# The first head's row of maxima, issued by ScalarE instead of SyncE

## The chip, the cores and the metric

One core of one Trainium2 chip runs the whole kernel. The metric is device time in microseconds (us) of one execution. Below, PE is TensorE, DVE VectorE, ACT ScalarE, POOL GpSimd and SP SyncE; "SPq" in a row is an instruction of SP's queue.

## The reference

Block-causal attention over 8 batches and 8 heads (576 positions, head size 64, blocks of 64), and then a gated product of four weight matrices:

```python
scores = scale * np.matmul(q, k.transpose(0, 1, 3, 2))        # [8, 8, 576, 576]
scores = np.where(block_i >= block_j, scores, -1000000000.0)   # blocks of 64 positions
scores = scores - np.max(scores, axis=-1, keepdims=True)
attn = np.exp(scores)
attn = attn / (np.sum(attn, axis=-1, keepdims=True) + 1e-09)
x = (attn @ v) as [4608, 512]
a = x @ w1                                                     # w1, w2: [512, 1024]
b = x @ w2
out = (a * b @ w3) @ w_out                                     # [1024, 1024], [1024, 512]
```

q, k and v are float32; the weights come as 64-bit numbers.

## The kernel before, in words

The heads are worked off in 32 pairs: four pairs for each batch, `NPAIR` = 4 and `NN` = 32. The two heads of a pair are j = 0 and 1; in tiles of 128 partitions, head j has 64 partitions of its own (`own[j]`) and uses the other 64 (`oth[j]`) for a second copy and for constants. Products are made in pieces of lower precision: each operand is split into a high and a low part.

**Scores.** For each head, the tile `qk[j]` has four slots of 576 columns. On the head's own partitions they hold q high, q low, k low, k high. On the other partitions, slots 0 and 2 get a copy of q high and k high by a transfer (L284, `qk<-qk`), and slots 1 and 3 constants (`const_rows`, L555: the mask's rows and a row of ones). A score tile (`s_tile`, L310, tile `s`) is two matmuls that add up: slot 2 times slot 0, then slot 3 times slot 1. One row of slot 1, on the partition `oth[j].start`, holds minus the maximum of every position's scores; met by the row of ones in slot 3, it subtracts the maximum within the second matmul. ACT then takes the exponential from PSUM (L318 in the first four pairs, tile `pe`; L325 to L330 later), and PE multiplies by v (L350 early, L374 later, tile `x`).

**The row of maxima.** `shift_mask(n)` makes it for pair n: PE multiplies a bf16 copy of q and k (`qd`, `kb`, L221 and L223; matmuls L235 into `mx`), DVE takes maxima of the rows (L239 to L244, tile `m`), PE transposes them (L246, `mt`), ACT negates them into `ms`, a tile of 9 partitions by 128 columns (L248). `shift(n, j)` (L257, `qk<-ms`) then moves head j's 9 by 64 numbers into the row of 576 in `qk[j]`, in 9 pieces of 256 bytes. For the first pair, n = 0, both heads' rows are moved right after each other at the end of `shift_mask`; for later pairs the second head's row follows in `prep_qk`.

**Weights.** While the first four pairs (`EARLY`) run, the weights are fetched in 21 pieces of 1 MB, in the order of `W_ORDER` ("o" is w_out, "3" is w3, "s" a piece of w1 or w2), into three raw buffers in turn (`fetch`, L184: `graw` and `wraw`). `assemble` turns the 64-bit numbers into float32: one pass on ACT (L195) and three on DVE (L196 to L198). A raw buffer is fetched into again only when its conversion is done. PE multiplies w3 by w_out once into one matrix (`gen_product`, L490, tile `w`). The gated product runs in blocks of 512 positions (`gen_moe`: L514 `ab`, then L533 `o`), filled in between the attention's steps, and continues after the last pair.

**The order of the work.** Two strings for each pair (`EARLY_PLAN`, `PLAN`) say in which order the steps are written down: S a score tile, V a part of the product with v, M a step of the next pair's maxima, A and B of preparing q and k, C a weight conversion, W a step of the product of weights, N, T and Q the end of a head. All transfers are issued from SP, in one queue. From the start to `start.close()` all five engines keep the order of the code (`manual_schedule`); this is the opening of pair 0 with its maxima, `const_rows`, the first conversion and `prep_qk`. After that a planner in the compiler orders each engine's instructions by priority and by times that it reckons for them. From pair 4 on PE keeps the order of the code again.

In the opening, the transfers on SP are: q and k of pair 0, constants, v, a first 1 MB piece of w_out, head 0's copies (L284), a first piece of w3, the two rows of maxima (L257), head 1's copies, a second piece of w3. ACT's order there is: `qd` for head 1, the high parts of head 0 (L280), `const_rows(0)`, `ms`, the first pass of the conversion (L195), v of head 0 (L296), the high parts of head 1 (L280); the first exponentials follow.

Of the kernel before, what the change touches and what calls it, by code (L numbers as in the profile page):

```python
# [7 lines left out]
F32 = mybir.dt.float32  # L8
# [10 lines left out]
BLK = 64  # L19
NB = S // BLK  # L20
# [57 lines left out]
def block_causal_attention__then__gated_mlp_kernel(ctx, tc, qkv, consts, ident_in, w1, w2, w3t, wout, out_t):  # L78
    nc = tc.nc
# [136 lines left out]
    ms_of = {}  # L216

    def shift_mask(n):
# [29 lines left out]
        nc.scalar.mul(out=ms[0:NB], in_=mt[0:NB, 0:P], mul=-1.0)  # L248
        ms_of[n] = ms
        shift(n, 0)  # L250
        if n == 0:
            shift(n, 1)
        yield

    def shift(n, j):
        row = qk[j][oth[j].start : oth[j].start + 1, 1, :].rearrange("p (i r) -> p i r", r=BLK)
        nc.sync.dma_start(out=row.bitcast(F32), in_=ms_of[n][0:NB, j * BLK : (j + 1) * BLK].bitcast(F32))  # L257

    def prep_qk(n, j):
        rqk = rqk_of[n].rearrange("p (t s) -> p t s", t=2)  # L260
        o, x = own[j], oth[j]
        if j == 1 and n:
            shift(n, 1)
        high, low = qk[j][o, 0::3, :], qk[j][o, 1:3, :]
        if n > EARLY:
            if j == 0:
                hf = tl["late"].tile([P, RQK], F32R, tag="hf", name=f"hf{n}")
                hf_of[n] = hf
                nc.scalar.copy(hf, rqk_of[n])  # L269
                yield  # L270
                lo = rqk_of[n].bitcast(F32R)
                nc.gpsimd.tensor_tensor(out=lo, in0=rqk_of[n], in1=hf, op=ALU.subtract)  # L272
                yield
            hf = hf_of[n].bitcast(F32).rearrange("p (t s) -> p t s", t=2)
            nc.sync.dma_start(out=high.bitcast(F32), in_=hf[o])
            nc.sync.dma_start(out=qk[j][x, 0::2, :].bitcast(F32), in_=hf[o])
            nc.sync.dma_start(out=low.bitcast(F32), in_=rqk[o])
            yield
            return
        nc.scalar.copy(high, rqk[o])  # L280
        yield
        if j == 0 and n:
            yield
        nc.sync.dma_start(out=qk[j][x, 0::2, :].bitcast(F32), in_=high.bitcast(F32))  # L284
        if n == 0:
            yield
        nc.vector.tensor_tensor(out=low, in0=rqk[o], in1=high, op=ALU.subtract)  # L287
        yield
# [416 lines left out]
```

## Time and profile before

| | us |
|---|---|
| median of 3 runs | 959.41 |
| lowest and highest | 957.72, 959.47 |
| the profiled execution's own time | 961.2 |
| its span, from first to last instruction | 959.4 |
| PE busy | 935.8 |
| DVE busy | 609.5 |
| ACT busy | 565.5 |

The mean granted clock of PE was 0.996 of full speed. In a row of the timeline the first number is the start, the second the length, then engine, line, operation, written and read tiles, how many were merged, and in brackets the engine's idle time before it and what ended that. A row of the chain of waits has start, length, and the work or transfer; a transfer's length there runs from its issue until the waiting engine could go on.

### The profile page before, as it was taken

What the parts mean: (1) busy time and instruction counts of PE and PEld (TensorE: products, weight loads), DVE (VectorE), ACT (ScalarE), POOL (GpSimd) and SP (SyncE); (2) the same over time, 40 slices, a digit from 0 to 9 for tenths busy, and PEclk for the clock granted to TensorE, in tenths of its full rate; (3) what the DMA queues carried; (4) which work ended last, traced back from release to release, by engine and by line L of the source; (5) the groups of instructions that cost most, each with busy time, mean ns of one, the idle gap of its engine ahead of it and who ended that gap; (6) DMA issues with size and microseconds to landing.
All of it is one profiled execution on the core that took longest, in us unless ns stands there. A gap on an engine that the chain in (4) does not pass through costs nothing.

```text
span 959.4 us, 13392 instructions
## 1 busy us (share of the span) xinstructions
PE 935.8 (98%) x4608; PEld 749.1 (78%) x4608; DVE 609.5 (64%) x1289; ACT 565.5 (59%) x1275; POOL 307.6 (32%) x254
## 2 busy tenths in 40 slices
PE   5899989999999999999999999999999999999998
PEld 3455567788888888888888888888888888888886
DVE  6899969766776677766776777667676776210010
ACT  5777666666666666666666666666666665222121
POOL 0000134352334234533453334334443443223120
PEclk9999989999999999999999999999999999999999
DMA  8788434455445544455445544554455442000001
GB/s 271 249 279 250 139 79 113 102 124 140 107 110 124 146 113 113 113 146 124 114 100 143 122 108 99 137 133 112 103 129 129 107 108 60 22 1 33 12 1 44
DMA packets 48823, 111.68 MB, mean 116 GB/s; under 512 B 5866, under 2 KB 14186, under 8 KB 48756
## 3 DMA queue, kind: packets, MB, share of 16 engines
q1 hardware_dynamic: 48756, 110.84, 44.4%
q8 instruction: 36, 0.59, 0.3%
q14 instruction: 31, 0.25, 0.1%
HBM read 50.51 MB, written 9.44 MB: 62 GB/s over the span
## 4 chain that ended last, share of the span: by engine, by line
PE 92%; DVE 3%; DMA 2%; ACT 2%; issue 1%; SPq 0%; DVEq 0%; ACTq 0%
PE ab L514 39%; PE o L533 21%; PE s L310 10%; PE x L374 9%; PE w L490 5%; PE mx L235 4%; PE x L350 3%; DMA rqk<-in_qkv 1%; DMA graw<-in_w3t 1%; DMA qk<-ms 0%; PE tot L391 0%; PE mt L246 0%; DVE m L242 0%; ACT qd L223 0%; DVE qk L287 0%
## 5 line engine op out<-in xcount | busy, mean ns | idle before, releaser
L523 POOL TENSOR_TENSOR gl<-a,gh 128x512 fp32r<-128x512 f32 x72 | 94.5, 1313 | 242.2 <-ACT gh L522 242.2
L310 PE MATMUL s<-qk 128*128 128x288 f32 (+4 forms) x768 | 158.8, 312 | 7.9 <-DMA qk<-ms 3.0
L310 PEld LDWEIGHTS s<-qk 128*128 128x128 f32 (+1 forms) x768 | 124.8, 182 | 41.1 <-issue 12.2
L242 DVE TENSOR_REDUCE m<-mx 128x1 f32<-128x512 f32 (+6 forms) x256 | 125.5, 503 | 30.9 <-PE mx L235 29.7
L329 ACT ACTIVATE ph<-s 128x448 fp32r<-128x448 f32 x224 | 85.9, 384 | 68.7 <-PE s L310 60.9
L521 DVE TENSOR_TENSOR a<-ab,a 128x512 f32<-128x512 f32 x72 | 49.6, 689 | 107.0 <-PE ab L514 104.4
L533 PE MATMUL o<-gh,wh 128*128 128x512 f32 x288 | 117.3, 407 | 0.0
L331 DVE TENSOR_TENSOR pl<-s,ph 128x448 fp32r<-128x448 f32 x168 | 81.5, 485 | 54.8 <-ACT s L330 54.4
L327 DVE TENSOR_TENSOR pl<-rsum,ph 128x288 fp32r<-128x288 f32 x112 | 56.5, 527 | 89.2 <-ACT ph L326 89.0
L533 PE MATMUL o<-gl,wh 128*128 128x512 f32 x288 | 112.8, 392 | 0.0
L533 PE MATMUL o<-gh,wl 128*128 128x512 f32 x288 | 112.6, 391 | 0.0
L272 POOL TENSOR_TENSOR rqk<-rqk,hf 128x1152 fp32r<-128x1152 f32 x27 | 72.2, 2673 | 86.8 <-ACT hf L269 86.2
L332 DVE TENSOR_TENSOR rsum<-s,rsum 128x448 f32<-128x448 f32 x224 | 92.9, 415 | 1.7
L374 PE MATMUL x<-ph,vs 128*128 128x128 f32 x336 | 87.5, 313 | 0.3 <-DVE ph L331 0.3
L522 ACT CAST gh<-a 128x512 fp32r<-128x512 f32 x72 | 44.4, 616 | 70.6 <-DVE a L521 69.5
L300 POOL TENSOR_TENSOR vs<-rv,vs 128x320 fp32r<-128x320 f32 x56 | 49.1, 878 | 113.2 <-ACT vs L299 108.0
L330 ACT ACTIVATE s<-s 128x448 f32<-128x448 f32 x224 | 85.4, 381 | 0.0
L235 PE MATMUL mx<-kb,qd 128*128 128x512 bf16 (+5 forms) x320 | 69.6, 295 | 6.9 <-DVE qd L223 5.2
L518 ACT COPY a<-ab 128x512 f32<-128x512 f32 x72 | 42.2, 586 | 55.0 <-PE ab L514 39.9
L374 PE MATMUL x<-pl,vs 128*128 128x128 f32 x280 | 71.3, 320 | 0.0
L374 PEld LDWEIGHTS x<-ph,vs 128*128 128x128 f32 x336 | 61.7, 190 | 12.2 <-DVE ph L331 3.2
L533 PEld LDWEIGHTS o<-gl,wh 128*128 128x128 f32 x288 | 54.0, 188 | 12.1
(128 smaller groups left out, 2094.3 us busy)
## 6 DMA issues: line engine op xcount, KB each, us to landing
qk<-hf SPq DMA_DIRECT2D x108, 288.0 KB
rqk<-in_qkv SPq DMA_DIRECT2D x31, 576.0 KB
qk<-rqk SPq DMA_DIRECT2D x54, 288.0 KB
rv<-in_qkv SPq DMA_DIRECT2D x31, 320.0 KB
out_t<-o SPq DMA_DIRECT2D x36, 256.0 KB
graw<-in_w3t SPq DMA_DIRECT2D x6, 1024.0 KB
graw<-in_w SPq DMA_DIRECT2D x5, 1024.0 KB
graw<-in_wout SPq DMA_DIRECT2D x3, 1024.0 KB
```

What stands on the lines that cost most here:

```text
L235: nc.tensor.matmul(sc, qd[:, i, :], kb[:, a:b], start=True, stop=True)
L242: nc.vector.reduce_max(m[:, col : col + 1], sc, axis=AX.X)
L272: nc.gpsimd.tensor_tensor(out=lo, in0=rqk_of[n], in1=hf, op=ALU.subtract)
L310: nc.tensor.matmul(t[ks, at : at + q1 - q0], qk[j][:, 2 + s, kr], qk[j][:, s, q0:q1], start=(s == 0), stop=(s == 1))
L329: nc.scalar.activation(h, sc, AF.Exp, scale=SCALE)
L330: nc.scalar.activation(sc, sc, AF.Exp, scale=SCALE)
L331: nc.vector.tensor_tensor(out=low, in0=sc, in1=h, op=ALU.subtract)
L332: nc.vector.tensor_tensor(out=r, in0=sc, in1=r, op=ALU.add)
L374: nc.tensor.matmul(xps[:, to : to + w], v[:, c, :], parts[s][:, a : a + w], start=(u < 2 and s == 0), stop=((u, s) in ((0, 1), (len(PV) - ...
L514: nc.tensor.matmul(acc[i], l[:, c, fs], r[c], start=(c == 0 and s == 0), stop=(c == NC - 1 and s == 2))
L523: nc.gpsimd.tensor_tensor(out=gl[f // 4][:, f % 4], in0=a32, in1=gh[f // 4][:, f % 4], op=ALU.subtract)
L533: nc.tensor.matmul(t, l[:, f, es], r[f // 4][:, f % 4], start=(f == 0 and s == 0), stop=(f == NF - 1 and s == 2))
```

## The change

`shift` picks the queue: for pair 0 and head 0 (`n + j == 0`) ACT issues the transfer, in all other cases SP as before. What is moved, from where and to where, is the same. In ACT's code the issue stands right after the instruction that makes `ms`.

```diff
     def shift(n, j):
         row = qk[j][oth[j].start : oth[j].start + 1, 1, :].rearrange("p (i r) -> p i r", r=BLK)
-        nc.sync.dma_start(out=row.bitcast(F32), in_=ms_of[n][0:NB, j * BLK : (j + 1) * BLK].bitcast(F32))
+        queue = nc.scalar if n + j == 0 else nc.sync
+        queue.dma_start(out=row.bitcast(F32), in_=ms_of[n][0:NB, j * BLK : (j + 1) * BLK].bitcast(F32))
```

## The prediction

> **What bounds the kernel now.** I read the page first, then PE's busy time in stretches, then the chain of waits through the opening, then the queues of SP, PE, ACT and DVE around 10 us, and last what the DMA engines moved there.
>
> ```profile
> span 959.4 us, 13392 instructions
> PE 935.8 (98%) x4608; PEld 749.1 (78%) x4608; DVE 609.5 (64%) x1289; ACT 565.5 (59%) x1275; POOL 307.6 (32%) x254
> ```
>
> PE is busy 98% of the span; a change that adds no matmul can win only PE's idle time, 959.4 - 935.8 = 23.6 us. The stretches say where it is idle (start:end, length, then busy us of PE, PEld, DVE, ACT, POOL, the granted clock, DMA share, GB/s):
>
> ```profile
> 48.00:60.00 12.00, 12.00 (x49) 7.05 (x49) 12.00 (x16) 8.48 (x15) 0.00 (x0) 1.00 0.99 294
> 60.00:80.00 20.00, 20.00 (x68) 10.50 (x66) 18.69 (x29) 14.02 (x23) 0.00 (x0) 1.00 0.68 221
> ...
> 100.00:120.00 20.00, 19.97 (x71) 10.96 (x69) 19.94 (x22) 13.48 (x24) 4.47 (x3) 1.00 0.34 118
> 200.00:500.00 300.00, 300.00 (x1590) 252.21 (x1589) 208.71 (x488) 195.37 (x472) 121.09 (x100) 1.00 0.50 121
> ```
>
> From 48 us on PE has hardly a gap. So whatever the change wins counts only if PE's matmul at about 48 us starts earlier; from there a shift is carried to the end. The chain of waits in that opening (start, length, what):
>
> ```profile
> 10.30 0.28 ACT ms L248
> 10.60 4.75 DMA qk<-ms
> ...
> 15.49 0.59 PE s L310
> 16.11 0.42 ACT pe_first L318
> ...
> 33.30 8.04 DMA graw<-in_w3t
> ...
> 47.78 1.13 PE w L490 x2
> ```
>
> The row of maxima is 4.75 us under way, and the chain runs through it. Farther on it leaves attention and runs through a fetch of w3 (33.30) and the conversion of those weights to PE's product with them at 47.78.
>
> **Why the row is late.** SP's queue, PE, and what the DMA engines moved from 12 to 16 us, in 40 slices of 0.1 us:
>
> ```profile
> 6.89 0.59 SPq L184 DMA_DIRECT2D graw<-in_w3t  x1
> 10.60 1.61 SPq L257 DMA_DIRECT2D qk<-ms  x2
> 13.96 0.68 SPq L284 DMA_DIRECT2D qk<-qk  x1
> 14.68 0.59 SPq L184 DMA_DIRECT2D wraw_first<-in_w3t  x1
> ```
>
> ```profile
> 12.80 0.82 PE L310 MATMUL s<-qk 128*128 128x288 f32 x2 [2.54 <-DMA qk<-qk]
> 15.49 0.82 PE L310 MATMUL s<-qk 128*128 128x288 f32 x2 [1.87 <-DMA qk<-ms]
> ```
>
> ```profile
> GB/s 358 348 358 389 317 328 241 197 220 192 133 108 102 46 20 31 20 20 31 20 31 20 20 31 20 20 15 0 0 0 0 0 92 161 346 138 253 138 253 184
> ```
>
> Ahead of the row on SP's queue stands a 1 MB fetch of w3, issued at 6.89. The rate falls from 350 GB/s to 46 at 13.4, as DMA engine after DMA engine finishes; then about 20 GB/s go on until 14.65, which I take for a single late engine, and 0.7 us after that stops the row is there (15.35). I read it so: the row's share on the late engine stands in that queue behind the fetch, and every share of the row must land. PE has done its first products of both score tiles by 12.80 + 0.82 = 13.62 and then waits 1.87 us for the row.
>
> **The change part by part.** Removed from SP: one issue, the first of two (1.61 us together, 0.8 each). The second head's row then issues at 10.60 rather than 11.4; still behind the fetch, it lands near 15.35, and nobody needs it before the second head's scores, which follow the whole of the first head. Nothing else on SP moves by this: its next DMA (13.96) waits for ACT's cast L280. Worth zero, covered by that wait.
>
> Added on ACT: that issue, behind `ms`, which ends at 10.58. No new instruction waits for it except the scores that waited already. ACT's queue, with what stands behind it:
>
> ```profile
> 11.29 1.12 ACT L195 ACTIVATE wbits_first<-graw 128x1024 f32<-128x1024 f32 x1 [0.72 <-DMA graw<-in_wout]
> ...
> 12.78 1.15 ACT L280 CAST qk<-rqk 64x1152 fp32r<-64x1152 f32 x1
> ...
> 21.01 1.16 ACT L195 ACTIVATE wbits<-wraw_first 128x1024 f32<-128x1024 f32 x1
> 22.74 0.64 ACT L399 COPY sm<-x 64x576 f32<-64x576 f32 x1 [0.57 <-PE x L350]
> ```
>
> ACT issues no DMA in this trace, so its price is bounded: not below 0.35 (the shortest issue of SP below), at most twice the 0.85 of SP's longest for this form, 1.70.
>
> ```profile
> L116 SPq DMA_DIRECT2D rqk<-in_qkv x4: 350/403/459, 0.7 to 26.2; - x4
> L257 SPq DMA_DIRECT2D qk<-ms x4: 709/772/850, 10.6 to 44.4; - x4
> ```
>
> I take 0.85, the same form: 10.60 + 0.85 = 11.45, so L195 starts 0.16 later (ends of the range: 0 and 10.60 + 1.70 - 11.29 = 1.01). The 0.72 us in which ACT waited for its weights covers the rest. The 0.16 passes to L280 (ends 14.09) and to SP's issue at 13.96; ACT is free before the first exponential, which comes at 13.62 + (16.11 - 15.49) = 14.24.
>
> Gained: on another queue the row doesn't stand behind the fetch. How early it lands is unknown: at the earliest like SP's idle queue at 13.96, whose bytes begin to flow at 15.2, 1.3 us later, with 0.7 to land: 10.60 + 1.3 + 0.7 = 12.6; at the latest as now, 15.35. Any time up to 13.62 does the same. I take that, as the late engine has only to put one 256-byte share between the fetch's: PE's second products start at 13.62, 1.87 us earlier. If the row is as late as now, the gain here is 0.
>
> The Trainium skill, DMA: Bandwidth & Descriptors, under Queues, rings and completion order, says that each DMA engine takes turns between the queue rows that have work, a packet (some 9 to 17 descriptors) at a time. By that the row would land near the early end, and the first rival below would have next to no chance; I leave it 15%, as no run here yet shows two queues at once.
>
> **What is late next.** From 16.11 to 20.7 nothing on ACT or PE waits for a transfer, so 1.87 is carried to about 19. Then ACT reaches L195 on `wraw_first` (21.01, would be 19.14), a weight fetch that SP issued at 14.68. When did it land?
>
> ```profile
> 15.00:16.00 1.00, 0.51 (x2) 0.50 (x2) 0.97 (x2) 0.00 (x0) 0.00 (x0) 1.00 0.70 157
> 16.00:17.00 1.00, 0.74 (x3) 0.42 (x2) 1.00 (x1) 0.87 (x3) 0.00 (x0) 1.00 1.04 204
> 17.00:18.00 1.00, 1.00 (x4) 0.96 (x4) 0.05 (x1) 1.00 (x2) 0.00 (x0) 1.00 0.90 261
> 18.00:20.00 2.00, 2.00 (x6) 1.03 (x6) 0.59 (x1) 2.00 (x4) 0.00 (x0) 1.00 1.13 390
> ...
> 15.28:32.40 17.12, 15.62 (x55) 9.63 (x55) 13.61 (x16) 13.62 (x23) 0.00 (x0) 1.00 0.98 342
> 32.40:35.20 2.80, 2.38 (x10) 1.23 (x9) 2.80 (x6) 2.25 (x4) 0.00 (x0) 1.00 0.33 94
> ```
>
> ```profile
> wraw_first<-in_w3t SPq DMA_DIRECT2D x1, 1024.0 KB
> qk<-qk SPq DMA_DIRECT2D x1, 288.0 KB
> qk<-ms SPq DMA_DIRECT2D x1, 2.2 KB
> ```
>
> The queue holds qk and w3, 1312 KB or 1.34 MB, from 15.2 (the row itself has 2.2 KB). By 18 us 157 + 204 + 261 = 622 KB have moved; the remaining 0.72 MB take 1.85 us at 390 GB/s: 19.85, and 0.7 to land, 20.5. A late engine adds to that, and it was there by 21.01. I take the middle, 20.75, plus 0.16 from ACT's issue: 20.9. L195 then ends at 20.9 + 1.16 = 22.07, and `sm` starts there rather than at 22.74: of 1.87 us some 0.67 are left. The DMA engines are full from 15.28 to 32.40 (0.98), so earlier issues bring nothing earlier there.
>
> ```profile
> 27.88 1.17 ACT L195 ACTIVATE wbits<-graw 128x1024 f32<-128x1024 f32 x1
> ...
> 32.03 1.21 DVE L198 SCALAR_TENSOR_TENSOR wo<-graw,wbits 128x1024 int32<-128x1024 int32 x1
> ```
>
> ACT then works without a gap up to L195 at 27.88 (its rows show no idle time from 22.74), and DVE converts those weights until 33.24, which frees the buffer for the fetch at 33.30. At this fetch the DMA engines had run empty (0.33 from 32.40), so it starts and lands 0.67 earlier, and so does PE at 47.78.
>
> **Sum.** +0 (SP) - 1.87 (PE's wait) + 1.20 (the wait for `wraw_first` that takes its place, ACT's 0.16 in it) = -0.67 us. The profiled execution took 961.2 us, with a span of 959.4; the median of the runs shown is 959.41. Against its own time 960.5, against the median 958.7. About 0.2%, 1.9 us, is what a measurement of this kernel can tell from no change, so the likeliest outcome is no measurable change.
>
> **The rivals.** *The row is as late as before* (15%). For it: the same 16 DMA engines move it, and the late one has to do the fetch anyhow. Against: nothing but its place in the queue explains 4.75 us for so few bytes. Then -0 + 0.16: 959.6. The Trainium skill, same page, under Issuing engines are not separate DMA queues, says that queues share the engines and a second issuer saves issue time alone; by that this row, already the first of SP's two, would win nothing. The trace here neither shows nor excludes it.
>
> *The whole 1.87 us arrives, and a little more* (17%, faster). PE waits between 15.5 and 48 us:
>
> ```profile
> PE w L490 <- DVE w L198: 2.0, 1, 2.0
> PE s L310 <- DMA qk<-ms: 1.9, 1, 1.9
> ...
> PE w L490 <- DVE wo L198: 0.4, 1, 0.4
> ```
>
> If `wraw_first` lands by about 19.3, or the planner puts `sm` ahead of it, 1.87 reaches 33.30, and the 0.4 at wo can go too: 959.4 - 2.3 = 957.1. Against: the byte count above. The most it could be is the waits shown, 4.3 us: 955.1.
>
> *The planner takes another order* (17%, slower). Only the opening up to `start.close()` is fixed on all engines by the code; behind it the planner orders instructions by times that it reckons itself, and a transfer moved from SP to ACT changes those. The place is ACT between 22.74 and 27.88, which has no gap: one L195 (1.16 us) taken ahead of the attention work, and its conversion on DVE (0.69 for L196 and twice the 1.21 of L198, at which I take L197 too, 3.1 us) ahead of the masks' maxima, delay PE by up to 3.1: 959.4 - 0.67 + 3.1 = 961.8. It decides from 2.6 us on. For it: DVE and ACT are the full engines there; against: PE holds other work to fill in.
>
> ```profile
> 19.41 0.69 DVE L196 TENSOR_SCALAR wbits<-wbits 128x1024 int32<-128x1024 int32 x1 [2.36 <-ACT wbits L195]
> ```
>
> **How the numbers follow.** Forecast 51% (958.7), row as late 15% (959.6), both without measurable change; faster 17%, slower 17%. So faster 0.17, same 0.66, slower 0.17. The range reaches from the faster rival to near the slower, 957.0 to 961.4. The forecast alone has 957.8 to 959.7: with `wraw_first` at 20.5 and no cost on ACT 0.9 + 0.16 gained and half a microsecond of spread, with 1.01 on ACT 0.2 lost.
>
> **What would show it.** Right: a DMA issue on ACT near 10.6; PE's second products at 13.6, no wait for qk<-ms there; ACT L195 on `wraw_first` still near 20.9 and now waiting for its DMA; the fetch of 33.30 at 32.6; PE w L490 at 47.1. Wrong: PE still waits for qk<-ms until 15.4; `sm` at 20.9; or a changed order of instructions after 18 us, with more idle time of PE between 22 and 131 us.

## The result, and the profile after

The changed kernel is slower: 966.60 us (median of 4 runs, 964.70 to 967.81) against 959.44 us (957.72 to 961.45) for the kernel before on the same chip, a ratio of 1.0072 [1.0052, 1.0091], 7.2 us. The prediction said 958.7 us, with a range up to 961.4, and gave "slower" 17%.

The profiled execution of the changed kernel took 964.7 us, 1.9 us less than its median, and that of before 1.8 us more than its own. So the two traces differ by only 3.5 us: they show where the time goes, the runs how much it is. (The granted clock was 0.998 in this execution and 0.996 in the other three runs; by an estimate, 0.002 of 965 us, the clock can make up to 1.9 us of the difference.) The first lines of the page after (29 matmul records are missing from this trace):

```profile
span 962.9 us, 13365 instructions
PE 935.2 (97%) x4579; PEld 747.2 (78%) x4608; DVE 610.2 (63%) x1289; ACT 566.2 (59%) x1275; POOL 308.4 (32%) x254
```

PE's idle time is 962.9 - 935.2 = 27.7 us, before it was 23.6. By stretches (columns as in the prediction), first before, then after:

```profile
16.00:48.00 32.00, 28.32 (x94) 15.37 (x93) 27.01 (x36) 23.70 (x38) 0.00 (x0) 1.00 0.83 276
48.00:100.00 52.00, 52.00 (x186) 28.30 (x186) 49.89 (x72) 38.52 (x65) 0.00 (x0) 1.00 0.85 263
100.00:200.00 100.00, 95.10 (x445) 70.65 (x444) 82.34 (x155) 67.09 (x148) 35.16 (x26) 0.97 0.41 104
```

```profile
16.00:48.00 32.00, 28.06 (x88) 15.52 (x89) 25.59 (x33) 22.06 (x36) 0.00 (x0) 0.95 0.83 274
48.00:100.00 52.00, 49.92 (x178) 26.71 (x178) 47.51 (x65) 37.46 (x63) 0.00 (x0) 1.00 0.78 246
100.00:200.00 100.00, 92.87 (x427) 66.70 (x429) 85.06 (x157) 67.90 (x146) 35.38 (x25) 1.00 0.42 110
200.00:500.00 300.00, 300.00 (x1584) 252.34 (x1596) 207.43 (x488) 195.25 (x474) 118.11 (x97) 1.00 0.50 120
```

From 48 to 100 us PE had no gap and now has 2.1 us of them; from 100 to 200 its idle time grows from 4.9 to 7.1; from 200 to 500 PE has no gap in either. From 16 to 100 us DVE and ACT are busy less: they get less done in the same time.

The opening, ACT's queue after (ACTq is an issue by ACT):

```profile
10.67 1.41 ACTq L258 DMA_DIRECT2D qk<-ms  x1
12.12 1.12 ACT L195 ACTIVATE wbits_first<-graw 128x1024 f32<-128x1024 f32 x1 [1.49 <-issue]
...
13.60 1.15 ACT L281 CAST qk<-rqk 64x1152 fp32r<-64x1152 f32 x1
15.65 0.89 ACT L319 ACTIVATE pe_first<-s 128x288 f32<-128x288 f32 x2 [0.89 <-PE s L311]
17.26 0.97 ACT L319 ACTIVATE pe_first<-s 128x448 f32<-128x448 f32 x2 [0.72 <-PE s L311]
18.79 0.43 ACT L319 ACTIVATE pe_first<-s 128x192 f32<-128x192 f32 x2 [0.56 <-PE s L311]
19.25 1.15 ACT L556 CAST qk<-cst 64x1152 fp32r<-64x1152 f32 x1
20.31 0.45 ACT L297 COPY ve<-rv 128x320 f32<-128x320 f32 x1
20.67 1.12 ACT L195 ACTIVATE wbits<-graw 128x1024 f32<-128x1024 f32 x1
```

PE's queue after, for the first score tiles:

```profile
11.33 0.58 PE L311 MATMUL s<-qk 128*128 128x288 f32 x1 [1.00 <-DMA qk<-qk]
15.03 2.73 PE L311 MATMUL s<-qk 128*128 128x288 f32 x7 [3.12 <-DMA qk<-ms]
```

Two things are to be seen. The row of maxima, issued by ACT at 10.67, is still late: PE waits for it until 15.03 (15.49 before). And the order has changed. PE does one first product and then wants the row, where before it did the first products of two tiles ahead of it. (The length of the wait, 3.12 us against 1.87, differs from execution to execution: here PE's first product starts at 11.33, before at 12.80. In a second trace of the changed kernel, that of `changed_again` below, it starts at 13.43, and the wait is 1.54 us.) On ACT all exponentials of the first head stand ahead of the constants for the second head (L556). Before, the constants and L195 stood between them:

```profile
16.11 0.71 ACT L318 ACTIVATE pe_first<-s 128x288 f32<-128x288 f32 x2 [2.17 <-PE s L310]
16.84 1.15 ACT L555 CAST qk<-cst 64x1152 fp32r<-64x1152 f32 x1
...
18.26 1.12 ACT L195 ACTIVATE wbits<-graw 128x1024 f32<-128x1024 f32 x1
19.28 0.84 ACT L318 ACTIVATE pe_first<-s 128x320 f32<-128x320 f32 x2
```

What that does shows on SP's queue. First before, then after:

```profile
18.02 0.35 SPq L116 DMA_DIRECT2D rqk<-in_qkv  x1
...
60.24 0.38 SPq L184 DMA_DIRECT2D wraw<-in_w  x1
...
128.43 0.44 SPq L116 DMA_DIRECT2D rqk<-in_qkv  x1
```

```profile
20.43 0.35 SPq L116 DMA_DIRECT2D rqk<-in_qkv  x1
21.35 0.38 SPq L184 DMA_DIRECT2D graw<-in_wout  x1
35.49 0.37 SPq L184 DMA_DIRECT2D graw<-in_w3t  x1
63.83 0.38 SPq L184 DMA_DIRECT2D wraw<-in_w  x1
134.98 0.45 SPq L116 DMA_DIRECT2D rqk<-in_qkv  x1
```

The fetch of pair 1's q and k (L116) goes into the buffer that holds the constants (`cst` and pair 1's `rqk` have the same tag in the same pool, so one buffer), so it can't start before ACT has read them for the last time. In both traces it starts 0.03 us after that cast ends: 16.84 + 1.15 = 17.99 and 18.02; 19.25 + 1.15 = 20.40 and 20.43. The view of SP's waits (after) puts this wait down to the copy of v that follows on ACT, which ended only at 20.31 + 0.45 = 20.76 and so can't have been it:

```profile
SPq L116 <- ACT ve L297: 4.6, 1, 4.6
```

The fetches of weights stand behind it in SP's queue: that of w3 goes from 33.30 to 35.49 (+2.2), the one at 60.24 to 63.83 (+3.6), and q and k at 128.43 to 134.98 (+6.6). SP's queue is not the only chain that is late, though. The conversion pass L195 on the first piece of w3 stands behind the same exponentials on ACT and starts at 20.67 instead of 18.26 (+2.4); its data had landed at 14.54. A raw buffer is fetched into again only after its conversion, so a late conversion delays fetches as well. PE comes to feel it where it needs converted w_out, 2.35 us where before it waited 0.42:

```profile
35.47 3.06 PE L491 MATMUL w<-wo,w_first 128*128 128x512 f32 x4 [2.35 <-DVE wo L198]
```

### The profile page after: what moved, and what is told of

Read it like the earlier page. It is cut to its first block, busy times and chain, and to the rows that moved or that the text cites. A ratio compares the mean times of both kernels' runs of the same rounds, so it can differ in the third digit from the quotient of the medians.

```text
span 962.9 us, 13365 instructions
## 1 busy us (share of the span) xinstructions
PE 935.2 (97%) x4579; PEld 747.2 (78%) x4608; DVE 610.2 (63%) x1289; ACT 566.2 (59%) x1275; POOL 308.4 (32%) x254
## 4 chain that ended last, share of the span: by engine, by line
PE 82%; DVE 2%; ACT 1%; issue 0%; DVEq 0%; ACTq 0%
PE ab L515 40%; PE o L534 21%; PE x L375 9%; PE s L311 9%; PE mx L235 3%; PE tot L392 0%; PE mt L246 0%; DVE rsum L333 0%; DVE a L522 0%; DVE pl L328 0%; DVE pl L332 0%; ACT ph L330 0%; DVE late_bits L197 0%; DVE late_bits L198 0%; DVE w2l L214 0%
## 5 line engine op out<-in xcount | busy, mean ns | idle before, releaser
L235 PE MATMUL mx<-kb,qd 128*128 128x64 bf16 (+7 forms) x291 | 58.3, 286 | 7.7 <-DVE qd L223 5.2
```

Source lines behind the costliest of these rows:

```text
L235: nc.tensor.matmul(sc, qd[:, i, :], kb[:, a:b], start=True, stop=True)
```

## The experiments

Two theories were put against each other: the time is lost by what the transfer itself does on ACT (its issue price), or by the order in which the planner now puts the instructions of the first four pairs. Comparing the two kernels' instructions engine by engine, PE's order differs in 149 places, DVE's in 56, ACT's within its first 121 instructions, SP's within its first 46; POOL's is the same, and nothing differs behind about 120 us.

To set the order by hand, the experiments chain the instructions of PE, DVE, ACT and SP by ordering edges without semaphores, from a list of instruction numbers for each engine. Line numbers in them are those of before.

**The changed kernel again**, with no edit.

```diff
 (the diff of the change, nothing else)
```

> The changed kernel itself, on the same chip as the three kernels beside it. Both theories: ratio 1.005 to 1.009 to the kernel before.

966.96 us, ratio 1.0072 [1.0052, 1.0092]. The loss repeats.

**The change with the order of before.**

```diff
-        nc.sync.dma_start(out=row.bitcast(F32), ...
+        (nc.scalar if n + j == 0 else nc.sync).dma_start(out=row.bitcast(F32), ...
...
+    for engine, numbers in ORDER.items():     # the order of the kernel before, 4 engines
+        for pair_ in zip(numbers, numbers[1:]):
...
+                tc.add_manual_dep(traced[b], traced[a].name, NOSYNC, reason="order")
```

> The changed kernel (the first head's row issued by ACT) with every engine's instructions held in the order that they have in the kernel before. If the planner's new order is what costs the time, this is within 1 us of before: ACT's issue takes 1.41 us, so its first conversion pass starts 0.8 us later, the row lands near 14.9 instead of 15.35, and the two nearly cancel (958.5 to 960.5). If ACT's issue itself costs the time, most of the 7 us stays: 963 to 967.

960.35 us, ratio 1.0004 [0.9996, 1.0013]: no loss, with the transfer on ACT.

```profile
10.64 1.31 ACTq L257 DMA_DIRECT2D qk<-ms  x1
11.99 1.12 ACT L195 ACTIVATE wbits_first<-graw 128x1024 f32<-128x1024 f32 x1 [1.38 <-issue]
```

```profile
15.14 0.82 PE L310 MATMUL s<-qk 128*128 128x288 f32 x2 [1.83 <-DMA qk<-ms]
```

The issue costs 1.31 us here and L195 starts 0.70 later than before (0.83 in the changed kernel), and PE's wait for the row is 1.83 instead of 1.87. Neither shows in the time. Nor does the chaining by edges, which this kernel has too.

**The order of the changed kernel, both rows on SP.**

```diff
+ORDER = {PE: ..., DVE: ..., ACT: ..., SP: ...}     # the order of the changed kernel; shift as before
```

> The kernel before (both rows issued by SP) with every engine's instructions held in the order that they have in the changed kernel. If the planner's order costs the time, this is as slow as the changed kernel, 964 to 968, ratio about 1.007. If ACT's issue costs it, this is within 1 us of before.

967.86 us, ratio 1.0082 [1.0068, 1.0097]. The loss comes without the change. The four cases together:

| | order of before | order of the changed kernel |
|---|---|---|
| first row on SP | 1 | 1.0082 [1.0068, 1.0097] |
| first row on ACT | 1.0004 [0.9996, 1.0013] | 1.0072 [1.0052, 1.0092] |

Its trace, whose execution took 2.0 us more than its median, has gaps in the same stretch, 3.3 us of them:

```profile
48.00:100.00 52.00, 48.72 (x168) 26.15 (x168) 45.88 (x63) 35.52 (x61) 0.00 (x0) 0.97 0.73 232
```

**The issue price alone: the second head's row, for which PE doesn't wait at that time, on ACT.**

```diff
-        nc.sync.dma_start(out=row.bitcast(F32), ...
+        (nc.scalar if n == 0 and j == 1 else nc.sync).dma_start(out=row.bitcast(F32), ...
+ORDER = ...                                        # the order of before
```

> The order of before, the first head's row issued by SP as before, and the second head's row, which nobody waits for at that time, issued by ACT instead: the price of the issue on ACT alone. ACT's L195 near 11.29 starts about 0.8 us later. If the order is the cause of the slower time: 0 to 0.8 us slower, 959.4 to 960.2. If ACT's issue is the cause: 963 to 967.

960.78 us, ratio 1.0014 [1.0002, 1.0025]. The issue takes 1.31 us again; it may cost 0.1%, about what can be told apart, and at most about a third of the loss by the upper end of the interval (0.25 of 0.72%).

**Which part of the order: pair 0 (to about 45 us) or what follows.**

```diff
+ORDER = ...     # both rows on SP; the changed kernel's order in pair 0, before's after it
```

> Both rows on SP, as before. Every engine has the changed kernel's order up to the end of the first pair (about 45 us) and the order of before from there. If the first pair's order carries the loss: the fetches of weights are 2.1 to 2.4 us late from 18 us on, as in the changed kernel's trace, and 2 to 2.5 us (ratio 1.002 to 1.003) arrive at the end. If the loss arises in later pairs' order: within 1 us of before. If all of it is in the first pair: 966 to 968.

964.35 us, ratio 1.0046 [1.0029, 1.0063]: more than the 0.2 to 0.3% expected. A part of it may be the clock. These six runs had a granted clock of 0.993 to 0.995, the 23 of before 0.996 to 0.998; by the means, 0.9945 and 0.9967, that is an estimated 2.1 us of the 4.4. Why their clock was lower was not found.

```diff
+ORDER = ...     # both rows on SP; before's order in pair 0, the changed kernel's after it
```

> Both rows on SP. Every engine has the order of before up to the end of the first pair (about 45 us) and the changed kernel's order from there: the other half of new_to_45us, which was 0.46% slower. If the two halves of the new order each carry a part of the loss and the parts add up: ratio 1.002 to 1.005, 2 to 4.5 us slower. If the later order costs only because the first pair came late: within 1 us of before.

963.64 us, ratio 1.0038 [1.0022, 1.0053]. Each half loses, and the halves add up: 0.46 + 0.38 = 0.84% against 0.82% for the whole order. PE's waits from 16 to 200 us in the second half's kernel show small ones (in all, times, longest) of which before has 0.2 us:

```profile
PE x L350 <- ACT pe L318: 1.7, 5, 0.5
PE mx L235 <- DVE m L242: 1.4, 2, 1.2
```

**Seven instructions of ACT alone.** Before's order with the constants, v's copy and L195 (176, 181, 185) moved behind the exponentials of the first head (212, 216, 243, 244), as the changed kernel has them; the three other engines as before.

```diff
-        ... 197, 204, 176, 181, 185, 216, 212, 243, 244, 220, ...
+        ... 197, 204, 212, 216, 243, 244, 176, 181, 185, 220, ...
```

> Both rows on SP and the order of before, but for seven instructions of ACT near 17 us, which have the changed kernel's order: the exponentials of the first head's last score tiles go ahead of the second head's constants, v and the second conversion pass (L555, L296, L195). If this place delays the chain of weights: the load of pair 1's q and k (18.0 us in before) issues near 20, the second conversion pass starts 2 us later, and 1.5 to 2.5 us arrive at the end. If those 2 us are made up before 48 us: within 1 us of before.

963.61 us, ratio 1.0037 [1.0024, 1.0050]: most of what pair 0's order costs (0.46%), and more than the 1.5 to 2.5 us expected. The rows of ACT, of SP, of PE's waits from 16 to 130 us, and two of the chain of waits, from an execution 2.0 us above the median:

```profile
20.00 1.15 ACT L555 CAST qk<-cst 64x1152 fp32r<-64x1152 f32 x1
21.41 1.12 ACT L195 ACTIVATE wbits<-graw 128x1024 f32<-128x1024 f32 x1
```

```profile
21.18 0.36 SPq L116 DMA_DIRECT2D rqk<-in_qkv  x1
...
36.56 0.37 SPq L184 DMA_DIRECT2D graw<-in_w3t  x1
```

```profile
PE w L490 <- DVE w_first L198: 3.8, 1, 3.8
PE w L490 <- DVE w L198: 2.4, 1, 2.4
```

```profile
24.55 1.24 DVE w_first L198
25.83 3.50 PE w L490 x4
```

The constants end at 21.15, SP's fetch of q and k starts at 21.18, and what stands behind it on SP is late: w3 by 3.3 us. So the place of one 1.15 us cast on ACT, before or behind the exponentials, sets when SP's queue goes on. PE then waits 6.2 us for converted weights, where before it waited 2.0 + 0.4; 3.8 us more, and the median is 3.1 us longer (by the ratio 3.6). But the longer of these waits, 3.8 us, is not SP's: it is for the conversion of the first piece of w3, whose pass L195 is one of the seven instructions and starts at 21.41 instead of 18.26, on data that SP had fetched well before the constants (issue at 7.03). So the loss belongs to the seven together; how it divides between the late conversion pass and the late queue was not separated.

**Is the row late because of the fetch ahead of it?** Both rows on SP, the 1 MB fetch of w3 issued behind them.

```diff
-        ... 133, 165, 166, 177, ...      # SP: fetch of w3, the two rows, the second head's copies
+        ... 165, 166, 133, 177, ...      # the order of before otherwise
```

> Both rows on SP and the order of before, but the fetch of w3 that stood ahead of them on SP's queue (6.89 us in before) now stands right behind them. If the row was late for standing behind that fetch: it lands by 13.3, and PE's second products start at about 13.5. If such a transfer takes 4.75 us by itself: still 15.3. The fetch comes 3 to 4 us later and what stands behind it some 1 to 1.5 us, so the time moves little: 958.5 to 961.

960.47 us, ratio 1.0000 [0.9987, 1.0013].

```profile
12.85 1.30 PE L310 MATMUL s<-qk 128*128 128x288 f32 x4 [2.40 <-DMA qk<-qk]
```

```profile
18.56 1.12 ACT L195 ACTIVATE wbits<-graw 128x1024 f32<-128x1024 f32 x1 [1.55 <-DMA graw<-in_w3t]
22.69 1.14 ACT L195 ACTIVATE wbits<-wraw_first 128x1024 f32<-128x1024 f32 x1 [1.60 <-DMA wraw_first<-in_w3t]
```

PE's wait for the row is gone: four products run on from 12.85. And nothing is gained, since ACT now waits 1.55 us for the fetch that was put back and 1.60 us for the next one.

**The row on ACT and the fetch behind the other row.**

```diff
+        (nc.scalar if n + j == 0 else nc.sync).dma_start(out=row.bitcast(F32), ...
-        ... 133, 165, 166, 177, ...      # SP
+        ... 166, 133, 177, ...           # 165 on ACT, the order of before otherwise
```

> The first head's row on ACT, the order of before, and the fetch of w3 behind the second head's row on SP. If a row on ACT's queue waits for transfers that SP issued before it, its late landing (about 14.9 in the changed kernel) goes with the fetch: 10.6 + 1.35 for ACT's issue + 1.3 + 0.7 = 14.0 or earlier. If it is ACT's own queue that is slow: still 14.9. Time 959 to 962.

959.88 us, ratio 0.9994 [0.9982, 1.0005].

```profile
12.86 0.82 PE L310 MATMUL s<-qk 128*128 128x288 f32 x2 [0.81 <-DMA qk<-ms]
```

```profile
21.66 1.13 ACT L195 ACTIVATE wbits<-wraw_first 128x1024 f32<-128x1024 f32 x1 [1.31 <-DMA wraw_first<-in_w3t]
```

With the fetch behind it, the same issue on ACT has its row there at 12.86 instead of 15.14. So the 1 MB fetch issued earlier is what delays it, on ACT's queue as on SP's. Of the 2.3 us won at PE, 1.3 are lost at its next products, which start at 15.25 and wait 1.57 us for ACT's first exponentials (0.26 with the fetch ahead): ACT's cast L280 ends only at 13.62 + 1.15 = 14.77. Then ACT waits for `wraw_first`.

**The row issued by GpSimd** (one run, 960.37 us).

```diff
+        (nc.gpsimd if n + j == 0 else nc.sync).dma_start(out=row.bitcast(F32), ...
+ORDER = ...                                        # the order of before
```

> The first head's row issued by GpSimd, which has nothing to do then, with the order of before and the fetch of w3 ahead of it on SP. If a transfer from any other queue waits until the DMA engines have worked off what SP issued before it: PE's second products start at 15 or later, as with SP and ACT. If GpSimd's queue is served in turn with SP's: near 13.6, without a wait for the row.

```profile
11.06 0.70 POOL L257 DMA_DIRECT2D qk<-ms  x1 [9.26 <-ACT ms L248]
```

```profile
15.25 0.82 PE L310 MATMUL s<-qk 128*128 128x288 f32 x2 [2.62 <-DMA qk<-ms]
```

A third queue doesn't bring the row earlier either, while the fetch is ahead.

**Two attempts at a faster version.** The first puts the second fetch of w3 ahead of the second head's copies, and ACT's constants into the gap before the exponentials.

```diff
-        ... 177, 217, ...                # SP
+        ... 217, 177, ...
-        ... 197, 204, 176, 181, ...      # ACT
+        ... 176, 181, 197, 204, ...
```

> The order of before with two gaps filled: on SP the second fetch of w3 (14.68 us in before) goes ahead of the second head's copies (13.96), for which SP waits for ACT; on ACT the second head's constants and v (L555, L296 at 16.84) go ahead of the first exponentials, into ACT's idle 2.17 us. If the chain of weight fetches sets the pace in the first 48 us, the DMA engines' pause at 14.65 to 15.2 goes, the conversion pass on wraw_first no longer waits, and 0.5 to 2 us arrive at the end: 957.5 to 959.5. If PE and ACT set it: no change.

960.70 us, ratio 1.0010 [1.0000, 1.0020].

```profile
15.94 1.15 ACT L555 CAST qk<-cst 64x1152 fp32r<-64x1152 f32 x1 [1.71 <-DMA qk<-ms]
```

The constants write to the slots into which the second head's row goes, and so had to wait for that transfer: the gap stayed empty. By the code they come after that row and write zeros over it, so in pair 0 the second head's maxima are moved for nothing (the softmax comes out the same without them), and yet the constants wait for them. No run leaves this transfer out. The second puts both rows ahead of both fetches on SP.

```diff
-        ... 133, 165, 166, 177, 217, ... # SP
+        ... 165, 166, 133, 217, 177, ...
```

> The order of before, but on SP: both rows, then both fetches of w3, then the second head's copies. It joins what fetch_behind_rows showed (the row lands at 13.4, PE's wait for it goes) with an earlier second fetch, whose lateness ate that gain there (ACT waited 1.60 us for it). If those two are all that stood against each other: PE's second products at 13.5, no wait on wraw_first, 1 to 2.5 us arrive: 957 to 959. If something else is late next: no change.

959.76 us, ratio 0.9999 [0.9988, 1.0010]. PE doesn't wait for the row, but ACT waits 0.79 us for `wraw_first` and then for PE:

```profile
24.37 0.64 ACT L399 COPY sm<-x 64x576 f32<-64x576 f32 x1 [1.35 <-PE x L350]
```

No version was measurably faster than the kernel before.

## Why the prediction was wrong, point by point

Two steps of the sum failed. It gives the row's early landing 1.87 us, and the row wasn't early; and it has no term for a new order of instructions, which the prediction names as a rival and prices at 3.1 us. With the order held the change makes no measurable difference (1.0004), where the sum has -0.67 us; the second is the whole loss.

**"On another queue the row doesn't stand behind the fetch."** This step failed: it is the first rival (15%). PE's wait for the row ends at 15.03 in the changed kernel, 15.14 with the old order, 15.25 from GpSimd, 15.49 from SP; with the fetch issued behind the row, at 12.86 from ACT. The small differences between the queues say nothing: in traces with both rows on SP behind the fetch, the first head's row lands between 14.43 (`new_order`) and 16.16 us (`new_to_45us`). The reading that the fetch of w3 delays the row was right; that a queue of its own would free it was not. The Trainium skill, DMA: Bandwidth & Descriptors, under Queues, rings and completion order, has each DMA engine take turns between queue rows, a packet of some 9 to 17 descriptors, at most 64, at a time; here, on the engines that carry both, the row's pieces of 256 bytes came behind those of the fetch that SP had issued 3.7 us ahead of it. By an estimate the fetch has 64 pieces of 1 KB for each of 16 engines: the traces agree with the Trainium skill if these are one packet and disagree if they are several, and no run here shows which. Under Issuing engines are not separate DMA queues the Trainium skill says that a second issuer saves issue time alone; that ACT's row, landing at 14.89 to 15.41 in three traces, lies within SP's 14.43 to 16.16 agrees with it. Here there was no issue time to save either.

**"I take 0.85" for ACT's issue.** It measured 1.41 us, inside the bounds 0.35 to 1.70 but near the upper end; the term is L195 from 11.29 to 12.12, +0.83 instead of +0.16, and the cast behind it, which ends at 13.60 + 1.15 = 14.75 instead of 14.09. That is later than the 14.24 at which the first exponential was to start, so with an early row ACT would not have been free, as the prediction has it. (In the nine traces in which ACT issues no transfer, L195 starts between 10.79 and 12.52, in most of them as its fetch lands; 0.83 is within that spread.) With the order held this made no measurable difference (1.0004), and at most 0.25% where nothing else was moved (the second row on ACT).

**"1.20, the wait for `wraw_first` that takes its place."** Right in kind, more than it said: where the row did come early, at 12.8 to 12.9, ACT waited 0.8 to 1.6 us for `wraw_first`, and 0.4 to 1.6 us for the fetch before it, and the time stayed at 0.9994 to 1.0000. These three kernels put the fetch back to get the row early, so part of the waits is their own; what a row that is early beside an unmoved fetch would gain, no run shows.

**"The planner takes another order" (17%, 961.8 us).** This is what happened, and by the four cases it decides alone: the same order without the change loses 0.82%, the change without it 0.04%. Two things of it were off. Its place: I took the opening as fixed to its end, and looked behind 22.74. The hand-written order holds only among the opening's own instructions. The exponentials of pair 0 are written down after `start.close()`, so the planner may put them before or behind the opening's last ones, and it moved them ahead of the second head's constants, at 16 to 20 us. Its size: I priced one weight conversion, 3.1 us. But the reordering runs on to about 120 us. The part in pair 0 costs 0.46% (4.4 us, perhaps half of it with the clock), and seven instructions of ACT alone 0.37%: the constants, which hold a buffer and with it SP's queue, and a conversion pass, both behind the exponentials. The part after pair 0 costs 0.38% (3.6 us), of which its trace shows 3.1 us in seven waits of up to 1.2 us. A sign of the first was in the trace of before: the fetch at 18.02 starts 0.03 us after the constants' cast ends, with 1 MB fetches queued behind it.

**"PE holds other work to fill in."** Wrong for the stretch from 48 us on: 2.1 us of gaps where there were none.

Open: why the planner chose this order. The times it reckons with are in no trace. PE's new order, both products of a score tile one after the other, is what one would write if the row were early; that is an inference. In pair 0 the late conversion pass and the late queue were not separated; of the second half's 0.38% no single move was isolated. In the trace of the changed kernel's order with both rows on SP, 968.1 - 939.6 = 28.5 us of PE are idle, 4.9 more than before; the other 3.8 us of its 8.7 are counted as PE's busy time, over the same 4608 matmuls. The granted clock accounts for an estimated 1.7 of them: by windows of 4 us it falls short of full speed by 5.2 us in three places of this trace (48 to 56, 136 to 144 and 184 to 188 us, lowest 0.57) and by 3.4 us in one of before (128 to 140, lowest 0.50). What the rest is wasn't found:

```profile
span 968.1 us, 13393 instructions
PE 939.6 (97%) x4608; PEld 750.1 (77%) x4608; DVE 610.3 (63%) x1289; ACT 566.4 (59%) x1275; POOL 308.1 (32%) x254
```

## What to carry to other kernels

Where a planner orders part of the program, an edit to one transfer is two changes, the transfer and a new order; compare the instruction orders first, and run the edit with the old order and the new order without the edit before explaining anything. Look for transfers that start right after some small instruction on another engine ends (here 0.03 us): a shared buffer there lets the place of a 1 us cast hold up a whole queue of fetches. A small transfer that must be early is put ahead of a large one in time, not on another queue, and what the large one then makes late has to be priced with it.

## What the runs showed of the hardware

- On the DMA engines that carry both, a small transfer from another queue did not pass a large one issued before it. The trace's semaphore records have each engine's share. In the changed kernel the last share of the fetch lands at 14.54 us and the last of ACT's row at 14.89; with the order of before, the last two at 13.86 and 14.84 and at 14.04 and 15.01; from GpSimd, the last at 14.96 and 15.12. With the fetch issued behind the row, the row has landed at 12.73.
- As a whole, the small transfer can land ahead of the large one: in `changed_again` at 15.41 against 15.76, and from SP's own queue in `new_order` at 14.43 against 15.65. The row's records have 10 landings, the fetch's 16; that the latest engine was then one that carries no piece of the row is a reading, as the records don't name the engines.
- The issue of this transfer (2.2 KB, 9 pieces) takes 1.31 to 1.42 us on ACT in four kernels, 0.70 to 0.86 on SP in pair 0 and 0.70 on GpSimd, and ACT does nothing else meanwhile. In all four SP issued the other row at the same time (10.66 and 10.67 us in the changed kernel), so how much of it is ACT's own isn't shown.
